# Longformer attention with a StarReLU feed-forward on one core: bias pieces in plain rows, and three transfers and turns moved

## The chip, the core and the metric

One Trainium2 chip, one of its cores. The metric is the device time of the program in microseconds, as the median of the runs; a profiled execution of the same program has its own time, which stands below beside its span.

## What is computed

For 8 batch elements of 8 heads, 576 positions and 64 columns, attention is taken within a window of 32 positions on either side and with 8 global positions; its output, with the heads side by side, is the input of a feed-forward of 512 to 2048 to 512 columns with the activation s * relu(h)^2 + b.

```python
scores = scale * np.matmul(q, k.transpose(0, 1, 3, 2))
mask = np.abs(pos[:, None] - pos[None, :]) <= window
mask = mask | is_global[:, None] | is_global[None, :]
...
attn = np.exp(scores)
attn = attn / (np.sum(attn, axis=-1, keepdims=True) + 1e-09)
x = np.matmul(attn, v)
...
h = x @ w_in
r = np.maximum(h, 0.0)
g = s * (r * r) + b
out = g @ w_out
```

The constant b reaches the output as b times the column sums of w_out. The kernel forms these sums by itself, and this is the "bias" of the title.

## The kernel before, in words

**Tiles and stages.** Two heads make a pair; there are 32 pairs, counted from 0, four to a batch element. Keys lie in 5 tiles of 120 rows plus the 8 global ones; each pair has two score steps (`qk(p, 0)` and `qk(p, 1)`, L652) whose products go through an exponential on ACT (L659) and a mask product on DVE (L660), and the products with V (`pvq`, L676) follow a step later. The feed-forward runs beside it on the same PE: `moe_quanta` is a generator whose steps (L771 into the hidden layer, L812 out of it) are put between the attention's steps by `run_pair`, eight steps to a pair. The work is bf16 with sums in f32.

**What sets the order.** All engines are in a manual schedule: each engine runs its instructions in the order in which the program writes them. Tables of (pair, step) say at which step a transfer or a copy is written. From pair 8 on PE's score work for pair p and the first half for pair p+1 stand together in `visit(p)`, which from pair 12 on is at step 3 of the pair.

**Q and K on their way.** For pairs 1 to 8 POOL loads K and Q with a cast (`load_kq`, L209) into a ring of five slots, and PE turns them (`trans`, L601). From pair 9 on SP loads K (`load_nat`, L236), ACT rounds it to bf16 (L247) and SP issues a DMA transposition (`turn_k`, L307) at step 5 of pair j-3; DVE then copies the global keys into it (`put_kq`, L566). From pair 18 on Q goes the same way (`load_q`, L264; `turn_q`, L312). All of these stand in SP's one queue in program order. At step 0 of pair 14 SP has the loads for pair 19, at step 4 those for pair 20, at step 5 the transposition of K of pair 17. A tile of K or Q rows has 64 f32 per row, so 256 bytes in one run. V of pairs 16 and later is loaded by POOL with a cast (L236, `vring`), its global rows by L555.

**The bias.** `w_out` is 4 MB in f32. `wpiece(j)` (L1146) has POOL load 512 KB, 128 partitions with a row of 1024 f32, into buffer `wst[j % 2]`; pieces 2 to 7 add themselves to what lies there (`accum_op`). Two pieces each are written at step 6 of pairs 11, 12, 14 and 15. `wadd` (L1152) then has DVE add the four halves in three additions in pair 17, and `bias` (L1158) multiplies the result with ones in pair 18.

**The other places.** `scatter(0, 1)` copies the global rows' results into place, eight small copies on POOL (L748); `load_kq(6)` is written behind it. `turned(trans_b, 5)` writes the turns of Q of pair 5 on PE and keeps their copy (L631) for later; it stands behind both score steps of pair 4. `gather(1)` (L405) fetches the global rows of K and Q of the second batch elements, two indirect transfers, and `load_kq(8)` stands behind it.

Of the kernel before, what the change touches and what calls it, by code (L numbers as in the profile page):

```python
# [9 lines left out]
FP32 = mybir.dt.float32  # L10
BF16 = mybir.dt.bfloat16
AF = mybir.ActivationFunctionType
OP = mybir.AluOpType
# [3 lines left out]
P = 128  # L17
# [3 lines left out]
DM, DF = 512, 2048  # L21
# [33 lines left out]
VGLOBAL = {  # L55
    8: (8, 3), 9: (8, 4), 10: (8, 7), 11: (9, 6), 12: (10, 6), 13: (11, 7), 14: (12, 7), 15: (13, 7),
}
KT0 = 16
NX = 3
N6 = NCH * KC // NJ  # L60
# [33 lines left out]
def kernel(  # L94
# [12 lines left out]
    nc = tc.nc  # L107
# [13 lines left out]
    stage = ctx.enter_context(tc.tile_pool(name="stage", bufs=1))  # L121
# [76 lines left out]
    wsum = wpool.tile([P, DM], FP32)  # L198
# [4 lines left out]
    w_in2 = moe_w_in.rearrange("(g p h) f -> p g h f", g=2, h=2)  # L203
    w_out2 = moe_w_out.rearrange("(a p t) n -> p a (t n)", p=P, t=2)

    def load_kq(p):
        bi, hp = divmod(p, 4)
        for t in "kq":
            nc.gpsimd.dma_start(  # L209
                out=six[t][:NP6, p % NR].rearrange("p h j d -> p h (j d)"),  # L210
                in_=src[t][bi, 2 * hp : 2 * hp + 2].rearrange("h (p j) d -> p h (j d)", j=NJ),
            )
# [186 lines left out]
    def gather(bb, ts="kq"):  # L399

        if bb not in gfs:
            gfs[bb] = globp.tile([P, 3, D], FP32, tag="gf", name="gf")
        for t in ts:
            i = "kqv".index(t)
            nc.gpsimd.indirect_dma_start(  # L405
                out=gfs[bb][:, i], out_offset=None,
                in_=src[t].rearrange("b h s d -> (b h s) d"),
                in_offset=IndirectOffsetOnAxis(ap=grow[bb][:], axis=0),
            )
# [97 lines left out]
    def flush():  # L507
        ops, later[:] = list(later), []
        for f in ops:
            f()  # L510
# [60 lines left out]
    both = [None]  # L571

    def trans(t, p):
        if p == 4:
            if t == "k":
                both[0] = ps_s.tile([P, 2, DM], FP32, tag="s", name="pst")
            ps = both[0][:, "kq".index(t)].bitcast(BF16)[:, 0:LQ]
        elif p < 5 or (t == "k" and p > 5):
            ps = bank("pst").bitcast(BF16)[:, 0:LQ]
        elif t == "k":  # L580
            ps = rings[-1].tile([P, DM], FP32, tag="moe", name="pst")[:].bitcast(BF16)[:, 0:LQ]
        else:
            both[0] = ps_s.tile([P, 2, DM], FP32, tag="s", name="pst")
            ps = both[0][:, 0].bitcast(BF16)[:, 0:LQ]
        if p >= NSIXQ:
            for c in range(NCH):
                nc.tensor.transpose(
                    ps[:, P * c : P * c + KC], qnat(p)[0:KC, P * c : P * c + P],
                    ident[0:KC, 0:KC],
                )  # L590
            return ps
        for j in range(NJ):
            n = N6 if j == NJ - 1 else NP6
            if t == "q" and p >= NSIX:
                nc.tensor.transpose(
                    ps[:, NP6 * j : NP6 * j + n],
                    qrow(p)[:n, j].rearrange("p h d -> p (h d)"), ident[:n, :n],
                )
                continue
            for hh in range(2):  # L600
                nc.tensor.transpose(  # L601
                    ps[D * hh : D * hh + D, NP6 * j : NP6 * j + n],
                    six[t][:n, p % NR, hh, j], ident[:n, :n],
                )
        return ps
# [138 lines left out]
    def scatter(bi, g=None):  # L744

        h = slice(0, 4) if g is None else slice(2 * g, 2 * g + 2)
        for i in range(NG):
            nc.gpsimd.tensor_copy(  # L748
                out=xt[:, h, S * (bi % NX) : S * (bi % NX) + S][:, :, ds(greg_p[i], 1)],
                in_=xgs[bi][:, h, i : i + 1],  # L750
            )
# [225 lines left out]
    def turned(f, p):  # L977
        ops = []
        f(p, ops)
        return ops[0]  # L980
# [113 lines left out]
    flush()  # L1094
    q_out()
    k_out()
    scatter(0, 1)
    load_kq(6)
    load_w_in(1, (1,))
    load_kq(7)  # L1100
    load_w_out(0)
# [15 lines left out]
    qk(4, 0)  # L1117
    lead()
    flush()
    steps0[0]()  # L1120
    qk(4, 1)
    flush()
# [3 lines left out]
    load_v(nc.sync, 7)  # L1126
    load_nat(nc.sync, "k", 9)
    load_q(9)
    q_out = turned(trans_b, 5)
    steps0[1]()  # L1130
    g_out = later.pop()
    q_out()
# [2 lines left out]
    flush()  # L1135
    cast_v(A, 4)
    gvall = const.tile([NG, (B - 2) * H * D], BF16)
    gather(1)
    load_kq(8)
    load_w_out(3)  # L1140
    quanta[0] = 31

    wst = [stage.tile([P, 2, DM], FP32, name=f"wst{i}", tag=f"wst{i}") for i in range(2)]

    def wpiece(j):
        nc.gpsimd.dma_start(  # L1146
            out=wst[j % 2][:].rearrange("p t n -> p (t n)"), in_=w_out2[:, j],
            **({"accum_op": OP.add} if j > 1 else {}),
        )

    def wadd(i):
        nc.vector.tensor_add(  # L1152
            out=wsum[:], in0=wsum[:] if i else wst[0][:, 0], in1=wst[(i + 1) // 2][:, (i + 1) % 2]
        )

    def bias():
        ps = bank("psb")
# [8 lines left out]
    for p in range(4, NPAIR):  # L1166
# [3 lines left out]
        def at(s, f, *a, ex=ex):  # L1170
            ex.setdefault(s, []).append(lambda: f(*a))
# [71 lines left out]
            at(4, steps[1])  # L1243
        elif p % 8 == 5 and 8 < p < NPAIR - 3:
            at(1, steps[1])
        if p in (11, 12, 14, 15):
            for j in range(2):
                at(6, wpiece, 2 * (11, 12, 14, 15).index(p) + j)
        if p == 17:
            for j in range(3):  # L1250
                at(2 * j + 2, wadd, j)
        if p == 18:
            at(2, bias)
        if p > 18 and hp in (0, 3) and held_rows:
# [46 lines left out]
```

## Time and profile before

| | |
|---|---|
| median of 3 runs | 343.88 us (342.3 to 344.29) |
| the profiled execution's own time | 343.63 us |
| its span, first to last instruction | 341.6 us |
| busy: PE, DVE, ACT, POOL | 322.5 (94%), 200.8 (59%), 199.7 (58%), 119.2 (35%) us |
| mean granted clock of PE | 0.98 |
| DMA | 125609 packets, 49.54 MB; 114072 of them under 512 B |

The page's times are microseconds from the first instruction. An engine's busy share is a mean over stages with different limits. A wait is time in which an engine stood idle, with what ended it. The queue q1 holds what SP issues, q0 what POOL issues; both use the same 16 DMA engines. A share of 16 engines can exceed 100%, since the time of every packet is counted from its start to its end.

### The profile page before, as it was taken

How to read it: one execution, taken by the hardware profiler on the slowest of the kernel's cores; microseconds unless marked ns; L12 is line 12 of the kernel's file. 1: busy time of each engine (PE TensorE's matmuls, PEld its weight loads, DVE VectorE, ACT ScalarE, POOL GpSimd, SP SyncE). 2: the span in 40 equal slices, each digit the busy share in tenths (PEclk: the TensorE clock that was granted, in tenths of full speed). 3: DMA queues.
4: the chain of work that ended last, by engine and by line, in shares of the span. 5: the costliest groups of instructions: out<-in, count | busy, mean ns of one | idle time of the engine just before them, and what ended most of it. 6: DMA issues, size and time to landing. Idle time of an engine off the chain costs nothing.

```text
span 341.6 us, 8778 instructions
## 1 busy us (share of the span) xinstructions
PE 322.5 (94%) x3403; PEld 169.5 (50%) x3403; DVE 200.8 (59%) x526; ACT 199.7 (58%) x335; POOL 119.2 (35%) x228
## 2 busy tenths in 40 slices
PE   7998999999999991699999999999999999999996
PEld 5754444444545450357744444444467544444444
DVE  6876686767786760347765676567656534423422
ACT  4777776578947871527865886588358505503600
POOL 7287624424235340080447605840670030000000
PEclk9999999999999997599999999999999999999999
DMA  8999999999999999899979999992950011011002
GB/s 145 195 179 219 203 208 216 191 205 167 251 196 178 111 195 181 147 173 162 165 154 249 189 179 187 238 166 53 203 114 2 2 68 57 0 61 63 0 34 92
DMA packets 125609, 49.54 MB, mean 145 GB/s; under 512 B 114072, under 2 KB 119640, under 8 KB 125560
## 3 DMA queue, kind: packets, MB, share of 16 engines
q1 hardware_dynamic: 94030, 27.49, 46.7%
q0 software_dynamic: 31184, 21.07, 37.3%
q8 instruction: 27, 0.44, 0.5%
q10 hardware_dynamic: 354, 0.43, 0.4%
q14 instruction: 14, 0.11, 0.1%
HBM read 42.28 MB, written 9.44 MB: 151 GB/s over the span
## 4 chain that ended last, share of the span: by engine, by line
PE 77%; DMA 9%; SPq 6%; POOL 3%; DVE 2%; issue 2%; ACT 1%; POOLq 0%; ACTq 0%
PE pso L812 35%; PE psh L771 31%; PE po L676 6%; DMA natq<-in_q_dram 4%; DMA sixk<-in_k_dram 3%; SPq L264 3%; SPq L236 2%; PE pss L652 2%; PE psw L652 1%; DMA natv<-in_v_dram 1%; PE pst L601 1%; DMA kt<-natb 1%; POOL xt L748 1%; DVE xt L723 1%; POOL gf L405 1%
## 5 line engine op out<-in xcount | busy, mean ns | idle before, releaser
L812 PE MATMUL pso<-wout_t,g 128*128 128x512 bf16 (+1 forms) x592 | 131.7, 378 | 0.0
L771 PE MATMUL psh<-xt,win 128*128 128x512 bf16 (+2 forms) x704 | 131.1, 341 | 0.3 <-DMA win<-in_moe_w_in_dram 0.3
L794 ACT ACTIVATE r<-psh 128x512 bf16<-128x512 f32 x144 | 85.7, 599 | 58.5 <-PE psh L771 53.2
L771 PEld LDWEIGHTS <-win 128*128 128x128 bf16 x704 | 63.2, 98 | 57.2 <-issue 0.6
L812 PEld LDWEIGHTS <-g 128*128 128x128 bf16 x592 | 56.5, 98 | 64.8 <-issue 3.0
L797 DVE TENSOR_TENSOR g<-r 128x512 bf16<-128x512 bf16 x144 | 61.0, 429 | 37.7 <-ACT r L794 35.3
L660 DVE TENSOR_TENSOR em<-em,mask 128x904 bf16<-128x904 bf16 x64 | 39.2, 616 | 35.1 <-ACT em L659 32.8
L659 ACT ACTIVATE em<-pss 128x840 bf16<-128x840 f32 (+1 forms) x38 | 33.5, 882 | 37.9 <-PE pss L652 37.6
L236 POOL DMA_DIRECT2D vring<-in_v_dram x33 | 30.6, 967 | 13.6 <-PE psh L771 8.7
L834 DVE SCALAR_TENSOR_TENSOR osb<-pso,sb,bias_row 128x512 f32<-128x512 f32 (+1 forms) x25 | 18.2, 728 | 28.7 <-PE pso L812 28.4
L723 DVE TENSOR_TENSOR xt<-po,rep 128x480 bf16<-128x480 f32 (+2 forms) x60 | 24.5, 450 | 3.8 <-ACT rep L733 3.8
L748 POOL COPY xt<-xg 128x4 bf16 (+1 forms) x72 | 16.4, 228 | 28.2 <-DVE xt L723 24.3
L652 PEld LDWEIGHTS <-kt 64*128 64x128 bf16 x384 | 12.1, 99 | 26.5 <-issue 12.3
L659 ACT ACTIVATE em<-psw 128x904 bf16<-128x904 f32 x23 | 21.2, 923 | 3.2 <-PE psw L652 3.2
L838 POOL DMA_DIRECT2D out_dram<-osb x16 | 9.1, 569 | 30.8 <-DVE osb L834 25.4
L676 PE MATMUL po<-em,vring 128*32 128x160 bf16 (+3 forms) x840 | 18.8, 224 | 0.7 <-issue 0.5
L322 POOL CAST vring<-natv 128x640 bf16<-128x640 f32 x10 | 8.0, 797 | 32.6 <-DMA natv<-in_v_dram 31.9
L247 ACT CAST natb<-natk 128x640 bf16<-128x640 f32 x22 | 15.9, 722 | 5.3 <-DMA natk<-in_k_dram 3.4
L652 PE MATMUL psw<-qt,kt 64*128 64x160 bf16 (+1 forms) x138 | 8.5, 230 | 10.1 <-DVE kt L566 10.0
L730 ACT ACTIVATE ln<-po 128x324 f32<-128x324 f32 (+1 forms) x30 | 12.9, 429 | 5.4 <-PE po L676 5.4
L652 PE MATMUL pss<-qt,kt 64*128 64x192 bf16 (+4 forms) x228 | 14.6, 240 | 1.5 <-ACT em L659 0.5
L676 PEld LDWEIGHTS <-vring 128*32 128x32 bf16 x896 | 14.6, 101 | 1.4 <-issue 1.3
(127 smaller groups left out, 253.5 us busy)
## 6 DMA issues: line engine op xcount, KB each, us to landing
natk<-in_k_dram SPq DMA_DIRECT2D x45, 150.0 KB
natv<-in_v_dram SPq DMA_DIRECT2D x28, 150.0 KB
natq<-in_q_dram SPq DMA_DIRECT2D x55, 75.0 KB
wst<-in_moe_w_out_dram POOLq DMA_DIRECT2D x8, 512.0 KB, 6.0
out_dram<-osb POOLq DMA_DIRECT2D x16, 256.0 KB, 4.1
natq<-in_q_dram SPq DMA_DIRECT2D x9, 288.0 KB
vring<-in_v_dram POOLq DMA_DIRECT2D x31, 75.0 KB, 5.3
out_dram<-osbh POOLq DMA_DIRECT2D x9, 256.0 KB
```

The lines of the kernel that those rows point to most:

```text
L236: eng.dma_start(out=dst[r : r + rows, n, c : c + nch, hh], in_=bass.AP(tensor=src[t].tensor, offset=o + c * KC * D, ap=[[D, rows], [KC * D ...
L652: nc.tensor.matmul(ps[:, hh, at : at + hi - lo], ktile[p][r, P * c : P * c + P], qbufs[p % 3][r, lo:hi], start=at == 0, stop=at + hi - lo ...
L659: nc.scalar.activation(em[:], ps[:, :, 0:n], AF.Exp, scale=SCALE)
L660: later.append(lambda: nc.vector.tensor_mul(em[:], em[:], masks[g]))
L676: nc.tensor.matmul(po[DH * j : DH * j + DH, a : a + n], view(vring[:, p % NVR, c, hh, part - 1 :], [2, DH]) if part else onesb[:], emt[(p, ...
L723: nc.vector.tensor_tensor(out=view(xt[:, 2 * g, x0 + t0 :], [NXT, 2], [w, runs], [1, w]), in0=view(po[:, STEP[blk] + col :], [STEP[blk], 2 ...
L748: nc.gpsimd.tensor_copy(out=xt[:, h, S * (bi % NX) : S * (bi % NX) + S][:, :, ds(greg_p[i], 1)], in_=xgs[bi][:, h, i : i + 1],)
L771: nc.tensor.matmul(psh[:, d0 : d0 + n], win_t[f // 8][:, a, 2 * P * (f % 8 // 2) :][:, 0 : 2 * P] .rearrange("p (x t) -> p t x", t=2)[:, f ...
L794: nc.scalar.activation(r[:], psh, AF.Relu)
L797: later.append(lambda g=g, r=r: nc.vector.tensor_mul(g[:], r[:], r[:]))
L812: nc.tensor.matmul(pso[:, 0:nn], gl[f][:, u * P : u * P + P], wout_t[:, f, n0 : n0 + nn], start=(f == 0), stop=(f == 15),)
L834: nc.vector.scalar_tensor_tensor(out=osb[:, 0:nn], in0=pso[:, 0:nn], scalar=s_bc, in1=bias_row[:, n0 : n0 + nn], op0=OP.mult, op1=OP.add,)
```

## The change

The eight pieces of 512 KB become sixteen of 256 KB, 128 partitions with a row of 512 f32, four to a set, in four buffers, and none adds itself to anything. A table `WPIECES` says at which (pair, step) a set is issued, and at which steps its four additions stand on DVE; there are fifteen additions, all into `wsum`. The first set is issued at step 1 of pair 11 and added in pair 12, the second at step 5 of pair 12 and added in pair 14, the third at step 4 of pair 14 and added in pair 15 and at step 0 of pair 16, the fourth at step 0 of pair 16 and added in pair 17. Besides, POOL's load of K of pair 6 stands ahead of `scatter(0, 1)`, that of Q behind it; the turns of Q of pair 5 stand between the two score steps of pair 4 and go into another PSUM tile; and `load_kq(8)` stands ahead of `gather(1)`.

```diff
--- before.py
+++ after.py
@@ -55,6 +55,12 @@
 VGLOBAL = {
     8: (8, 3), 9: (8, 4), 10: (8, 7), 11: (9, 6), 12: (10, 6), 13: (11, 7), 14: (12, 7), 15: (13, 7),
 }
+WPIECES = [
+    ((11, 1), ((12, 0), (12, 1), (12, 2), (12, 4))),
+    ((12, 5), ((14, 0), (14, 1), (14, 2), (14, 4))),
+    ((14, 4), ((15, 5), (15, 6), (15, 7), (16, 0))),
+    ((16, 0), ((17, 1), (17, 2), (17, 4), (17, 5))),
+]
 KT0 = 16
 NX = 3
 N6 = NCH * KC // NJ
@@ -203,9 +209,9 @@
     w_in2 = moe_w_in.rearrange("(g p h) f -> p g h f", g=2, h=2)
     w_out2 = moe_w_out.rearrange("(a p t) n -> p a (t n)", p=P, t=2)
 
-    def load_kq(p):
+    def load_kq(p, which="kq"):
         bi, hp = divmod(p, 4)
-        for t in "kq":
+        for t in which:
             nc.gpsimd.dma_start(
                 out=six[t][:NP6, p % NR].rearrange("p h j d -> p h (j d)"),
                 in_=src[t][bi, 2 * hp : 2 * hp + 2].rearrange("h (p j) d -> p h (j d)", j=NJ),
@@ -580,7 +586,11 @@
         elif t == "k":
             ps = rings[-1].tile([P, DM], FP32, tag="moe", name="pst")[:].bitcast(BF16)[:, 0:LQ]
         else:
-            both[0] = ps_s.tile([P, 2, DM], FP32, tag="s", name="pst")
+            if p == 5:
+                both[0] = ps_o.tile([P, 2 * DM], FP32, tag="o", name="pst")
+                both[0] = both[0][:].rearrange("p (h x) -> p h x", h=2)
+            else:
+                both[0] = ps_s.tile([P, 2, DM], FP32, tag="s", name="pst")
             ps = both[0][:, 0].bitcast(BF16)[:, 0:LQ]
         if p >= NSIXQ:
             for c in range(NCH):
@@ -1094,8 +1104,9 @@
     flush()
     q_out()
     k_out()
+    load_kq(6, "k")
     scatter(0, 1)
-    load_kq(6)
+    load_kq(6, "q")
     load_w_in(1, (1,))
     load_kq(7)
     load_w_out(0)
@@ -1117,6 +1128,7 @@
     qk(4, 0)
     lead()
     flush()
+    q_out = turned(trans_b, 5)
     steps0[0]()
     qk(4, 1)
     flush()
@@ -1126,7 +1138,6 @@
     load_v(nc.sync, 7)
     load_nat(nc.sync, "k", 9)
     load_q(9)
-    q_out = turned(trans_b, 5)
     steps0[1]()
     g_out = later.pop()
     q_out()
@@ -1135,23 +1146,22 @@
     flush()
     cast_v(A, 4)
     gvall = const.tile([NG, (B - 2) * H * D], BF16)
+    load_kq(8)
     gather(1)
-    load_kq(8)
     load_w_out(3)
     quanta[0] = 31
 
-    wst = [stage.tile([P, 2, DM], FP32, name=f"wst{i}", tag=f"wst{i}") for i in range(2)]
-
-    def wpiece(j):
-        nc.gpsimd.dma_start(
-            out=wst[j % 2][:].rearrange("p t n -> p (t n)"), in_=w_out2[:, j],
-            **({"accum_op": OP.add} if j > 1 else {}),
-        )
-
-    def wadd(i):
-        nc.vector.tensor_add(
-            out=wsum[:], in0=wsum[:] if i else wst[0][:, 0], in1=wst[(i + 1) // 2][:, (i + 1) % 2]
-        )
+    wst = [stage.tile([P, DM], FP32, name=f"wst{i}", tag=f"wst{i}") for i in range(4)]
+
+    def wpieces(j):
+        for i in range(4):
+            nc.gpsimd.dma_start(out=wst[i][:], in_=w_out2[:, 2 * j + i // 2, DM * (i % 2) :][:, 0:DM])
+
+    def wadd(j, i):
+        if j + i == 0:
+            return
+        a, b = (wsum, wst[i]) if j or i > 1 else wst[0:2]
+        nc.vector.tensor_add(out=wsum[:], in0=a[:], in1=b[:])
 
     def bias():
         ps = bank("psb")
@@ -1243,12 +1253,12 @@
             at(4, steps[1])
         elif p % 8 == 5 and 8 < p < NPAIR - 3:
             at(1, steps[1])
-        if p in (11, 12, 14, 15):
-            for j in range(2):
-                at(6, wpiece, 2 * (11, 12, 14, 15).index(p) + j)
-        if p == 17:
-            for j in range(3):
-                at(2 * j + 2, wadd, j)
+        for j, (x, adds) in enumerate(WPIECES):
+            for i, y in enumerate(adds):
+                if y[0] == p:
+                    at(y[1], wadd, j, i)
+            if x[0] == p:
+                at(x[1], wpieces, j)
         if p == 18:
             at(2, bias)
         if p > 18 and hp in (0, 3) and held_rows:
```

POOL's order from the scatter of the third batch element (pairs 12 to 16) on, before: `wst` are the bias pieces, `vring<-in_v_dram` V of pairs 16, 17 and 18, `vring<-gvall` their global rows.

```order
L1146 DMA wst_1041<-in_moe_w_out_dram 128x1024
L1146 DMA wst_1042<-in_moe_w_out_dram 128x1024
L236 DMA vring<-in_v_dram 120x5x64 x2
L1146 DMA wst_1041<-in_moe_w_out_dram 128x1024
L1146 DMA wst_1042<-in_moe_w_out_dram 128x1024
L555 DMA vring<-gvall 8x5x128
L236 DMA vring<-in_v_dram 120x5x64 x2
L1146 DMA wst_1041<-in_moe_w_out_dram 128x1024
L1146 DMA wst_1042<-in_moe_w_out_dram 128x1024
```

And now:

```order
L242 DMA vring<-in_v_dram 120x5x64 x2
L1158 DMA wst_1041<-in_moe_w_out_dram 128x512
L1158 DMA wst_1042<-in_moe_w_out_dram 128x512
L1158 DMA wst_1043<-in_moe_w_out_dram 128x512
L1158 DMA wst_1044<-in_moe_w_out_dram 128x512
L561 DMA vring<-gvall 8x5x128
L242 DMA vring<-in_v_dram 120x5x64 x2
L561 DMA vring<-gvall 8x5x128
L1158 DMA wst_1041<-in_moe_w_out_dram 128x512
L1158 DMA wst_1042<-in_moe_w_out_dram 128x512
L1158 DMA wst_1043<-in_moe_w_out_dram 128x512
L1158 DMA wst_1044<-in_moe_w_out_dram 128x512
```

The two pieces that stood between the scatter and V of pair 16 are now four ahead of the scatter; the third set stands where the second pair of pieces stood; the fourth stands behind the global rows that it stood ahead of.

DVE's order in pair 14, before: `qt` and `kt` are the copies for the visit of the same pair, `g` the squares of the feed-forward, `em` the mask products.

```order
L566 COPY qt_117<-gqt_121 128x5x8
L797 TENSOR_TENSOR g_2490<-r 128x512
L797 TENSOR_TENSOR g_2514<-r 128x512
L566 COPY kt<-gkt 128x5x8
L797 TENSOR_TENSOR g_2526<-r 128x512
L797 TENSOR_TENSOR g_2535<-r 128x512
L660 TENSOR_TENSOR em_2543<-em_2543,mask_449 128x840
L660 TENSOR_TENSOR em_2556<-em_2556,mask_441 128x904
```

And now:

```order
L572 COPY qt_117<-gqt_121 128x5x8
L807 TENSOR_TENSOR g_2499<-r 128x512
L1164 TENSOR_TENSOR wsum<-wsum,wst_1041 128x512
L807 TENSOR_TENSOR g_2524<-r 128x512
L572 COPY kt<-gkt 128x5x8
L1164 TENSOR_TENSOR wsum<-wsum,wst_1042 128x512
L807 TENSOR_TENSOR g_2537<-r 128x512
L1164 TENSOR_TENSOR wsum<-wsum,wst_1043 128x512
L807 TENSOR_TENSOR g_2547<-r 128x512
L670 TENSOR_TENSOR em_2555<-em_2555,mask_449 128x840
L670 TENSOR_TENSOR em_2568<-em_2568,mask_441 128x904
```

One addition stands ahead of the copy of K, three ahead of the mask products.

## Rows read from the trace of the kernel before

**Rows 1.** PE's waits: engine, line and tile, what ended the wait: total, times, longest.
```profile
PE psw L652 <- DVE kt L566: 10.0, 1, 10.0
...
PE pst L601 <- DMA sixk<-in_k_dram: 0.4, 1, 0.4
```
**Rows 2.** The chain that ended last: start, us, engine, tile, line, count.
```profile
96.17 0.20 PE psw L652 x6
96.37 0.67 PE po L676 x36
...
136.14 3.04 DMA kt<-natb
...
139.44 0.56 PE psw L652 x5
139.99 1.17 PE po L676 x38
141.16 9.11 PE pso L812 x32
...
242.88 7.01 PE pso L812 x32
```
**Rows 3.** Timeline of SP's queue, 72 to 142: start, us, line, transfer, count.
```profile
110.85 2.69 SPq L236 DMA_DIRECT2D natk<-in_k_dram  x2
113.58 11.30 SPq L264 DMA_DIRECT2D natq<-in_q_dram  x4
124.93 5.84 SPq L236 DMA_DIRECT2D natk<-in_k_dram  x2
130.88 5.09 SPq L264 DMA_DIRECT2D natq<-in_q_dram  x4
...
138.63 1.92 SPq L264 DMA_DIRECT2D natq<-in_q_dram  x4
```
**Rows 4.** Timeline of POOL, 100 to 142; in brackets idle time before, and what ended it.
```profile
99.73 0.72 POOL L322 CAST vring<-natv 128x640 bf16<-128x640 f32 x1 [5.32 <-DMA natv<-in_v_dram]
...
113.41 0.85 POOL L1146 DMA_DIRECT2D wst<-in_moe_w_out_dram  x1 [3.45 <-DMA wst<-in_moe_w_out_dram]
...
125.54 0.85 POOL L1146 DMA_DIRECT2D wst<-in_moe_w_out_dram  x1 [3.08 <-DMA natq<-in_q_dram]
```
**Rows 5.** Slices of 1 us: length, PE busy, granted clock, DMA share, GB/s.
```profile
131.00:132.00 1.00, 0.00 (x0) 0.86 1.17 196
...
145.00:146.00 1.00, 1.00 (x5) 0.82 0.93 211
```
**Rows 6.** DMA queues in 106 to 109: packets, MB, share of 16 engines.
```profile
q0 software_dynamic: 139, 0.50, 86.9%
```
**Rows 7.** DMA queues in 88 to 89.
```profile
q0 software_dynamic: 62, 0.25, 86.2%
```
**Rows 8.** DMA queues in 310 to 330.
```profile
q1 hardware_dynamic: 235, 0.45, 5.9%
```
**Rows 9.** DMA queues in 138 to 144.
```profile
q1 hardware_dynamic: 3679, 0.90, 89.8%
```
**Rows 10.** All DMA packets in 123 to 126.
```profile
DMA packets 2171, 0.51 MB, mean 168 GB/s; under 512 B 2137, under 2 KB 2145, under 8 KB 2171
```
**Rows 11.** All DMA packets in 117 to 119.
```profile
DMA packets 39, 0.10 MB, mean 51 GB/s; under 512 B 15, under 2 KB 15, under 8 KB 39
```
**Rows 12.** Timeline of DVE, 106 to 128.
```profile
120.52 0.18 DVE L566 COPY kt<-gkt 128x40 bf16<-128x40 bf16 x1 [0.50 <-DMA kt<-natb]
```
**Rows 13.** Instructions that touch `wst`: duration in ns, smallest, median, largest.
```profile
L1152 DVE TENSOR_TENSOR wsum<-wsum,wst x2: 681/684/686, 153.5 to 155.7; 128x512 f32<-128x512 f32 x2
```
**Rows 14.** Slice of 4 us: length, busy PE, PEld, DVE, ACT, POOL, clock, DMA share, GB/s.
```profile
116.00:120.00 4.00, 4.00 (x25) 1.93 (x24) 3.48 (x10) 2.67 (x6) 0.73 (x1) 1.00 0.57 81
```
**Rows 15.** DMA issues of the page: count, KB each, median us to landing.
```profile
wst<-in_moe_w_out_dram POOLq DMA_DIRECT2D x8, 512.0 KB, 6.0
```
**Rows 16.** DMA issues in 114 to 120.
```profile
vring<-in_v_dram POOLq DMA_DIRECT2D x2, 75.0 KB, 12.5
```

## The prediction

> Pairs are counted from 0 here, as in the code: the title's 6th pair is pair 5. Each four of the sixteen pieces are called a set.
>
> **What bounds the kernel now.** The page first: PE is busy for 94% of the span, so only what stops PE, or slows it, costs time. The second view is PE's list of waits [rows 1]: one wait of 10.0 us is nearly all that there is to take, and the next that bears on the change is 0.4 us. The third is the chain of waits followed back from that stop [rows 2]: `psw` at 139.44 waits for K of pair 17. SP issued its DMA transposition at 136.14, the data took 3.04 us, DVE's small copy about 0.2 us. PE had nothing to do from about 129.46 (139.44 less 9.98), so an issue by 126.2, 9.9 us earlier, would have cost nothing.
>
> Why was SP so late? Its own timeline [rows 3] shows what stands ahead of that issue: the K and Q loads of pairs 19 and 20. Four Q issues take 1.92 us where nothing disturbs them (the row at 138.63); here they took 11.30 and 5.09 us, and two K issues 2.69 and 5.84 us. An issue that takes so long, with no other engine named as the one waited for, goes into a queue that does not drain. POOL's timeline [rows 4] shows what shares the 16 DMA engines with it: accumulating 512 KB pieces of `moe_w_out`, three of the six between 113 and 126 (the first and the last stand in the rows), the first of them held up until an earlier piece of its buffer had landed.
>
> The clock comes last [rows 5]: it falls from 1.00 to 0.50 of full speed (2.4 to 1.2 GHz) inside the slice 131 to 132, when PE had stood still since 129.46, and is back inside 145 to 146, with PE at work since 139.44. So nearly 6 us of work after the stop run at half clock.
>
> **The change, part by part.**
>
> *Accumulation removed, pieces halved.* In 106 to 109 the software queue moved 139 packets, all but a few of 4 KB, at 86.9% of 16 engines [rows 6]: 0.869 x 16 x 3 us / 139 = 300 ns each, accumulating. In 88 to 89 4 KB without accumulation took 0.862 x 16 x 1 us / 62 = 222 ns [rows 7]. The new pieces are 2 KB rows without accumulation, and no row has such a load. Bounds: 80 ns, a packet of an output store with rows of 2 KB (0.059 x 16 x 20 us / 235, [rows 8]), and 222 ns, if half the bytes were no cheaper. I take 111 ns, half of the 4 KB row, which is the nearest: same tensor, same direction, same queue. 1 MB then costs all engines 256 x 300 / 16 = 4.8 us before and 512 x 111 / 16 = 3.6 us now (2.6 to 7.1).
>
> *What that does to SP's queue.* From 110.85 to 136.14, 25.3 us, SP pushes four times 300 KB, 4,800 packets of 256 B. The hardware queue alone moves 3,679 packets in 6 us, 613 in one [rows 9]; beside a V load with its 128 B packets the two queues move 2,171 in 3 us, 724 in one [rows 10]. Before: four accumulating pieces (512 packets of 300 ns over 16 engines), 9.6 us; the V load's 1,200 packets beside as many of SP's, 2,400 / 724 = 3.3 us; the other 3,600 alone, 5.9 us; together 18.8 us. Some 6.5 us are left over, and part of them is a stretch in which hardly anything moves, 39 packets in 117 to 119 [rows 11]. After: only the third set lies there, 3.6 us, since the fourth is released by additions that stand from step 5 of pair 15 on, from about 123. With 3.3 and 5.9 us that is 12.8 us: the turn of K is issued at 123.6, 2.6 us before it is needed. With the dear packet (222 ns) it is issued at 127.1, 0.9 us late; if the thin stretch returns with 4 us, at 127.6, 1.4 us late; with both, 5 us late. I take no stop, **-9.98 us**, because the nearest row for the packet leaves a margin, and keep the 5 us for the range.
>
> *The sets' places.* The second set now falls near 97 instead of 103, into a stretch that the queues already fill. Most exposed is the K copy of pair 16 at 120.52, which waited 0.50 us for its transposition [rows 12]; what lay ahead of that was the old second megabyte and the first accumulations of the third. Both now come earlier or cost less, so I cost the move at nothing; without that cover this copy is late first, a visit of PE before the old stop.
>
> *Clock.* Without the stop nothing lets it fall. At half clock `psw`, `po` and 32 `pso` took 0.56 + 1.17 + 9.11 us, the same blocks at full clock 0.20 + 0.67 + 7.01 [rows 2]: **-2.96 us**, and nothing of it if 5 us of stop stay.
>
> *Fifteen additions instead of three.* Twelve more at 0.68 us [rows 13] are 8.2 us of DVE, in pairs 12 and 14 to 17; DVE has 3.48 of 4 us filled in the fullest stretch there [rows 14]. PE feels it only where a copy that it waits for stands behind an addition; one addition stands ahead of the K copy in pair 14. I take **+0.3 us**, half of one addition, between 0 and 2.5 us (one set's four with no gap for them). On POOL, eight more issues of at most 0.85 us; behind the second set's four, which wait for DVE, stand the cast of V and a scatter, and POOL stood idle for 5.32 us before that cast [rows 4]. That idle time hides them: 0.
>
> *K of pair 6 ahead of the scatter.* PE waited 0.4 us for it [rows 1]; POOL now issues it before eight column copies. **-0.4 us**, between 0 (the weights issued ahead of it in the same queue land first) and 0.8 us (as much again behind it). *Q of pair 5 turned between the score steps of pair 4; K and Q of pair 8 ahead of the gather.* The transposition fills a hole of PE, but DVE copies its result in the same place, behind the second mask product, so PE meets the next wait: 0, between -0.4 and +0.4 us. The gather moves behind two loads of 144 KB and is rounded much later.
>
> **Sum.** 341.6 - 9.98 - 2.96 - 0.4 + 0.3 = 328.6 us of span. The profiled execution took 343.63 us, 2.03 us over its span, which makes **330.6 us**. It lay 0.25 us under the median of the runs shown, 343.88.
>
> The trace has 6.0 us from issue to landing of a plain 512 KB piece [rows 15]. A rule of the Trainium skill speaks against cutting it in two: "DMA: Bandwidth & Descriptors", sections "Anatomy of one DMA — SWDGE (gpsimd) path" and "Rules for kernel authors", asks for transfers of 1 MiB and more and counts about 2.0 us fixed plus the bytes at 436 GB/s for each. As an estimate from that page, four pieces of 256 KB one after another take 10.4 us where two of 512 KB take 6.4 us, and the sum would grow by what DVE waits for them, as in the third rival.
>
> **The rivals.**
> 1. *The stop shrinks but stays.* Nothing in the trace names the cause of the thin stretch [rows 11]; if the V load makes it, and not the accumulation, it returns. With the dear packet as well: 5 us of stop and the clock's 3 us: 330.6 + 8 = **338.6 us**, or anything from 333.5 to 341.
> 2. *The change does not do what it says*: SP is late by its own small packets, and the new pieces hold the engines as long as the old. That is so from 150 ns for half the bytes if the thin stretch stays in full. For it: 4,800 packets are there as before. Against it: 111 ns as half of the plain row. Only the 0.4 us and the additions are left: **343.5 us**.
> 3. *Slower: DVE becomes the wait.* DVE works in order, and a set's additions stand ahead of mask products and K copies. The third set's last piece is issued near 114 and its first addition stands near 123: from about 9 us to landing on, DVE stops, and ACT and PE behind it. For it: a 75 KB software load took 12.5 us in this stretch [rows 16]. Against it: 6.0 us for 512 KB [rows 15]. At 12.5 us it is 3.5 us for each of the last two sets, with the old stop only moved: 343.5 + 7 = **350 us**.
>
> By the page's 10.4 us the third rival would be just past its point.
>
> **How the numbers follow.** Forecast (328.5 to 333.5): 0.66, as the margin of 2.6 us hangs on one price taken between bounds. The first rival 0.16, the second 0.10, the third 0.08. A measurement of this kernel tells some 0.5%, 1.7 us, from no change. Faster by more: forecast and first rival, 0.82; the same: the second, 0.10; slower: the third, 0.08. The range takes in the forecast and the first rival and leaves out the other two: 328.5 to 341.
>
> **What would show it.** Right: PE's list without the 10.0 us; four Q issues of SP near 2 us in 113 to 131; the turn of K issued near 124; the clock at 1.00 from 30 to the end; PE's 0.4 us for K gone. Wrong: a `psw` that still waits for a K copy, at this pair or a neighbour; DVE rows that wait for `wst`; a PE wait for a copy that an addition held up.

## The result, and the profile after

Over four runs the change took 334.37 us in the median (331.49 to 339.33) beside 344.0 us of the kernel before: a ratio of 0.9702, 95% interval 0.9613 to 0.9791. It is faster, as forecast; the time forecast was 330.6 us, the range 328.5 to 341. The profiled execution took 331.49 us, with a span of 329.9. A second series gave 334.24 us (six runs, 330.99 to 339.78), ratio 0.9685 [0.9628, 0.9742]. Two single times near 339.5 us are left out of these ratios, and no profile shows one of them.

First PE's list of waits in the change, of the same columns as [rows 1]:

```profile
PE psw L662 <- DVE kt L572: 1.6, 2, 1.4
...
PE pss L662 <- DVE g L807: 0.8, 1, 0.8
PE psw L662 <- DVE gqt L539: 0.6, 1, 0.6
```

The 10.0 us of [rows 1] are gone, and so are the 0.4 us of `pst`. The three lines shown are new, all short. The first is two waits, for K of pair 9 near 67 and for K of pair 10 near 75; the 0.8 us stand at 34.05, where PE is no later than before (34.03); the 0.6 us stand near 105 and are taken up in run 7. SP's timeline shows why the long one went; it answers to [rows 3]:

```profile
112.99 1.00 SPq L242 DMA_DIRECT2D natk<-in_k_dram  x2
114.04 1.97 SPq L270 DMA_DIRECT2D natq<-in_q_dram  x4
116.05 1.04 SPq L242 DMA_DIRECT2D natk<-in_k_dram  x2
117.21 3.99 SPq L270 DMA_DIRECT2D natq<-in_q_dram  x4
121.36 1.92 SPq L313 DMA_TRANSPOSE kt<-natb  x1
```

The same four issues that took 2.69, 11.30, 5.84 and 5.09 us now take 1.00, 1.97, 1.04 and 3.99. The transposition of K of pair 17 is issued at 121.36 instead of 136.14. POOL's timeline, beside [rows 4], shows when the third and the fourth set are issued:

```profile
113.19 0.58 POOL L1158 DMA_DIRECT2D wst<-in_moe_w_out_dram  x1 [6.58 <-DVE wsum L1164]
...
117.58 0.54 POOL L1158 DMA_DIRECT2D wst<-in_moe_w_out_dram  x1 [1.90 <-DVE wsum L1164]
...
126.06 0.58 POOL L1158 DMA_DIRECT2D wst<-in_moe_w_out_dram  x1 [4.87 <-DVE wsum L1164]
```

Between 118 and 126 no piece is issued: the fourth set's buffers come free only with the third set's additions. The stretch 117 to 119, in which 39 packets moved before [rows 11], now moves 667:

```profile
DMA packets 667, 0.51 MB, mean 253 GB/s; under 512 B 577, under 2 KB 577, under 8 KB 667
```

The clock, in the windows that answer to [rows 5] (length, busy PE, PEld, DVE, ACT and POOL, clock, DMA share, GB/s), stays at 1.00:

```profile
130.00:132.00 2.00, 1.84 (x56) 1.20 (x56) 0.73 (x3) 1.29 (x2) 1.43 (x2) 1.00 1.14 253
132.00:146.00 14.00, 13.84 (x135) 8.67 (x135) 10.74 (x27) 8.92 (x17) 8.60 (x17) 1.00 1.44 204
```

Where the 11.7 us of span came from is read off PE's timeline, by the starts of the score blocks. The rows of the change, with idle time before them in brackets:

```profile
65.15 0.36 PE L662 MATMUL pss<-qt,kt 64*128 64x92 bf16 x6
66.92 0.37 PE L662 MATMUL psw<-qt,kt 64*128 64x160 bf16 x6 [1.42 <-DVE kt L572]
...
104.14 0.36 PE L662 MATMUL pss<-qt,kt 64*128 64x92 bf16 x6
105.10 0.37 PE L662 MATMUL psw<-qt,kt 64*128 64x160 bf16 x6 [0.60 <-DVE gqt L539]
...
130.31 0.36 PE L662 MATMUL pss<-qt,kt 64*128 64x92 bf16 x6
130.50 0.36 PE L662 MATMUL psw<-qt,kt 64*128 64x160 bf16 x6
```

Before, these six stood at 66.22, 66.69, 103.67, 103.86, 129.10 and 139.44, the last two being the stop:

```profile
129.10 0.36 PE L652 MATMUL pss<-qt,kt 64*128 64x92 bf16 x6
139.44 0.56 PE L652 MATMUL psw<-qt,kt 64*128 64x160 bf16 x6 [9.98 <-DVE kt L566]
```

So PE is 1.07 us ahead at 65.15 and gives that back at once (+0.23 at 66.92), is 0.47 us behind at 104.14, 1.24 us behind after the wait at 105.10, 1.21 us behind at 130.31. From there to the next block it needs 0.19 us where it needed 10.34: 10.15 us gained. After that block it gains 2.76 more (8.94 ahead, 11.7 at the end). All of that is there by the next block (138.48 instead of 150.20), the stretch that ran at half clock before, so it is the clock. Sum: 1.21 - 10.15 - 2.76 = -11.7 us.

### The profile page after: what moved, and what is told of

Its sections match the earlier page's. It is cut to its first block, busy times and chain, and to the rows that moved or that the text cites. A ratio compares the mean times of both kernels' runs of the same rounds, so it can differ in the third digit from the quotient of the medians.

```text
span 329.9 us, 8781 instructions
## 1 busy us (share of the span) xinstructions
PE 315.7 (96%) x3366; PEld 168.4 (51%) x3403; DVE 208.1 (63%) x538; ACT 199.6 (61%) x335; POOL 121.6 (37%) x236
## 4 chain that ended last, share of the span: by engine, by line
PE 80%; DMA 9%; ACT 4%; DVE 3%; issue 2%; SPq 1%; ACTq 0%; DVEq 0%
PE psh L781 34%; PE pso L822 32%; PE po L686 6%; DMA natk<-in_k_dram 5%; DMA kt<-natb 4%; PE pss L662 3%; ACT em L669 2%; PE pst L611 1%; PE psw L662 1%; PE psf L985 1%; SPq L242 1%; ACT r L804 1%; DVE xt L733 1%; PE psf L964 1%; PE pst L605 0%
## 5 line engine op out<-in xcount | busy, mean ns | idle before, releaser
L781 PE MATMUL psh<-xt,win 128*128 128x512 bf16 (+4 forms) x688 | 129.7, 340 | 1.1 <-issue 0.3
L822 PE MATMUL pso<-wout_t,g 128*128 128x512 bf16 (+1 forms) x573 | 126.4, 373 | 2.4 <-issue 2.1
L242 POOL DMA_DIRECT2D vring<-in_v_dram x33 | 29.4, 895 | 12.6 <-PE psh L781 7.2
L758 POOL COPY xt<-xg 128x4 bf16 (+1 forms) x72 | 17.2, 238 | 12.7 <-DVE xt L733 8.7
L1158 POOL DMA_DIRECT2D wst<-in_moe_w_out_dram x16 | 8.9, 573 | 19.6 <-DVE wsum L1164 16.5
```

The costliest lines, as they stand in the source:

```text
L242: eng.dma_start(out=dst[r : r + rows, n, c : c + nch, hh], in_=bass.AP(tensor=src[t].tensor, offset=o + c * KC * D, ap=[[D, rows], [KC * D ...
L758: nc.gpsimd.tensor_copy(out=xt[:, h, S * (bi % NX) : S * (bi % NX) + S][:, :, ds(greg_p[i], 1)], in_=xgs[bi][:, h, i : i + 1],)
L781: nc.tensor.matmul(psh[:, d0 : d0 + n], win_t[f // 8][:, a, 2 * P * (f % 8 // 2) :][:, 0 : 2 * P] .rearrange("p (x t) -> p t x", t=2)[:, f ...
L822: nc.tensor.matmul(pso[:, 0:nn], gl[f][:, u * P : u * P + P], wout_t[:, f, n0 : n0 + nn], start=(f == 0), stop=(f == 15),)
```

## The experiments

Eleven runs followed: 1 to 4 on one chip, 5, 6, 7 and 10 on a second, 8, 9 and 11 on a third, each group beside the kernel before.

**1. The accumulation alone, at the old places** (the kernel before with one line out; a later piece of a buffer then overwrites the earlier one):

```diff
-            **({"accum_op": OP.add} if j > 1 else {}),
```

> The kernel before with the accumulation alone taken away: the same eight pieces of 512 KB, at the same steps, with the same waits for the earlier piece of the buffer, each overwriting what lay there (so the bias is that of the last pieces alone). My theory, that the accumulating packets hold the DMA engines and SP's queue behind them: PE's 10.0 us wait for K of pair 17 and the half clock are gone, span 328 to 332 us, time 330 to 334 us, a 4 KB packet of these pieces near 220 ns instead of 300. Rival, that the smaller pieces or the new steps did it: the wait stays at 8 us or more, time 341 to 345 us.

Measured: 337.54 us (336.96 to 338.11), ratio 0.9803 [0.9736, 0.987]. The stop is still there, shorter, and the transposition is issued at 124.20:

```profile
PE psw L652 <- DVE kt L566: 4.7, 2, 4.4
```
```profile
118.62 5.41 SPq L264 DMA_DIRECT2D natq<-in_q_dram  x4
124.20 2.57 SPq L307 DMA_TRANSPOSE kt<-natb  x1
```

The chain of this profile gives the transposition's time from issue to landing, 8.77 us where it was 3.04 before [rows 2]:

```profile
124.20 8.77 DMA kt<-natb
```

Plain pieces bring 6 us of the gain, not all of it: between the two expectations. The turn is issued 2 us before the 126.2 that the prediction asks for, and PE still stops for 4.43 us.

**2. The three other moves alone** (the change with the old bias load, whose core is):

```diff
-            nc.gpsimd.dma_start(out=wst[i][:], in_=w_out2[:, 2 * j + i // 2, DM * (i % 2) :][:, 0:DM])
+            out=wst[j % 2][:].rearrange("p t n -> p (t n)"), in_=w_out2[:, j],
+            **({"accum_op": OP.add} if j > 1 else {}),
```

> The kernel before with the three moves (K of pair 6 ahead of the scatter, Q of pair 5 between the score steps of pair 4, K and Q of pair 8 ahead of the gather) and the old bias. My theory: the moves are worth next to nothing: the first wait for K of pair 6 (0.4 us) goes, PE is up to 0.9 us ahead near 44 us and 0.3 to 0.5 us behind the kernel before from about 75 us on, where a copy of K of pair 9 is late; the 10 us wait stays; time 342.5 to 345 us. Rival, that the moves carry a share of the gain: 340 us or less.

Measured: 344.14 us (342.6 to 344.88), ratio 0.9982 [0.9947, 1.0018]: no difference. The new wait at 67 is there as in the change, so it belongs to the moves. It is for K of pair 9, the first that SP turns (the expectation has that wait near 75):

```profile
67.02 0.37 PE L662 MATMUL psw<-qt,kt 64*128 64x160 bf16 x6 [1.56 <-DVE kt L572]
```

**3. The bias pieces alone** (the change with those three moves undone):

```diff
...
-    load_kq(6, "k")
     scatter(0, 1)
-    load_kq(6, "q")
+    load_kq(6)
...
-    q_out = turned(trans_b, 5)
     steps0[0]()
...
+    q_out = turned(trans_b, 5)
     steps0[1]()
...
-    load_kq(8)
     gather(1)
+    load_kq(8)
```

> The changed kernel with its three moves undone. My theory: the bias pieces carry the whole gain: no wait of 10 us, clock 1.0, span 328.5 to 330.5 us, time within 1.5 us of the changed kernel and rather below it, since the 1.4 us wait near 75 us goes with the moves. Rival, that the moves were needed: 334 us or more in its best run.

Measured: 335.95 us (332.89 to 337.61), ratio 0.9745 [0.9655, 0.9836]: the whole gain, within the intervals. Its profiled span of 334.0 us is not the 328.5 to 330.5 expected. PE waits there 2.3 us for the first weights (`win`, at 28.36), with the clock at 0.50 at 31, and so begins the score block at 31.06 that the change begins at 29.34. It has no wait near 67, but at the place of the 0.60 us a longer one:

```profile
107.52 0.37 PE L658 MATMUL psw<-qt,kt 64*128 64x160 bf16 x6 [2.50 <-DVE gqt L539]
```

**4. The new steps with accumulation** (the change's pieces, steps and buffers; sets two to four accumulate, three additions on DVE):

```diff
+                **({"accum_op": OP.add} if j else {}),
...
-        if j + i == 0:
+        if j < 3 or i == 0:
             return
-        a, b = (wsum, wst[i]) if j or i > 1 else wst[0:2]
+        a, b = (wsum, wst[i]) if i > 1 else wst[0:2]
```

> The changed kernel with the sets 2 to 4 adding themselves to their buffers in the DMA and three additions on DVE at the end: the same sixteen pieces, buffers and steps of the change, waits for the landed piece instead of for DVE. My theory: accumulation costs about a third to a half more per packet, and the wait of PE for a K copy in pairs 14 to 17 is back with 4 to 10 us, the clock falls again, time 337 to 345 us. Rival, that the steps and the four buffers made the gain: no wait over 2 us, time 330 to 335 us.

Measured: 339.7 us (339.44 to 341.15), ratio 0.9878 [0.9809, 0.9948], inside the theory's 337 to 345. The stop at the old block is back, with its clock (the block takes 0.56 us again):

```profile
137.11 0.56 PE L662 MATMUL psw<-qt,kt 64*128 64x160 bf16 x6 [4.75 <-DVE kt L572]
```

The pieces did not go out at the change's times, though. An accumulating set waits for no addition on DVE, so the third and the fourth are issued 6 and 7 us earlier than in the change (113.19 and 126.06), and both lie ahead of the turn of K:

```profile
107.11 3.60 POOL L1158 DMA_DIRECT2D wst<-in_moe_w_out_dram  x4
118.84 3.63 POOL L1158 DMA_DIRECT2D wst<-in_moe_w_out_dram  x4
```

Their packets are dear as well. In 114 to 116 the software queue moved 188 packets and 0.35 MB, about 2 KB each, at 94.6% of 16 engines: 0.946 x 16 x 2 us / 188 = 161 ns, so 512 x 161 / 16 = 5.2 us for a megabyte.

Runs 1 and 4 with the two kernels make a table of medians in us (not all of one series, so good to about 1 us):

| | accumulating | plain |
|---|---|---|
| old steps | 344.0 | 337.5 |
| new steps | 339.7 | 334.4 |

The upper row differs by one line of code: plainness is worth 6.5 us there. The right column differs in the steps, in the wait for DVE, in the size of a piece and in the moves, together 3.1 us; for the last two, runs 2, 3 and 5 show nothing clear of noise. The lower row is not plainness alone, since its sets are issued at different times.

**5. Eight pieces of 512 KB at the new places** (plain, the same steps and fifteen additions):

```diff
...
-        for i in range(4):
-            nc.gpsimd.dma_start(out=wst[i][:], in_=w_out2[:, 2 * j + i // 2, DM * (i % 2) :][:, 0:DM])
+        for i in range(2):
+            nc.gpsimd.dma_start(out=wst2[i][:].rearrange("p t n -> p (t n)"), in_=w_out2[:, 2 * j + i])
```

> The change with eight plain pieces of 512 KB (rows of 4 KB) in place of sixteen of 256 KB (rows of 2 KB), at the same steps, with the same fifteen additions. Theory (what counts is that nothing accumulates and that each megabyte comes when the queue has room; the packets that carry the small pieces are of 4 KB as well, about 170 ns each near 102): the waits for K stay under 2.5 us and the time is 331 to 338 us, that of the change. Rival (the small pieces carry the gain that a plain load of the old pieces did not give): the stop at K of pair 16 or 17 comes back with 2 to 5 us and the time is 336 to 341 us.

Measured: 335.65 us (333.53 to 337.41), ratio 0.9774 [0.9714, 0.9834], which overlaps the change's in the same series. The waits for K stay under 2 us, as the theory has it, and no stop at K of pair 16 or 17 comes back: small pieces aren't what took it away. Its profile waits 1.49 us for Q of pair 18. The ratios leave room for some 3 us against the larger pieces.

**6. The change once more**, not edited.

> The change once more, for the spread of its times beside the other runs of this call. Theory (a wait near 105 that is of another length in each execution, with a fall of the clock when it is long): median 331 to 336 us, single times up to 339, and a wait for K of pair 14 of between 0 and 3 us in the profile. Rival (the spread is of the chip and not of this wait): the wait is 0.6 us again, whatever the time.

Measured: 334.24 us, as told above; this profiled execution took 335.76 us with a span of 334.1, 4.2 us longer than the first. PE's rows show where:

```profile
104.69 0.36 PE L662 MATMUL pss<-qt,kt 64*128 64x92 bf16 x6
107.59 0.37 PE L662 MATMUL psw<-qt,kt 64*128 64x160 bf16 x6 [2.55 <-DVE gqt L539]
117.58 0.36 PE L662 MATMUL pss<-qt,kt 64*128 64x92 bf16 x6
```

At 107.59 it is 2.5 us behind the first execution, at 117.58 4.2 us: the clock fell behind the stop (length, busy PE, clock, DMA share, GB/s):

```profile
109.00:112.00 3.00, 3.00 (x8) 0.50 1.40 141
```

Of the 4.2 us, 0.55 were lost before the block (104.69 for 104.14), 1.95 are the longer wait (2.55 us for 0.60) and 1.70 the clock behind it. So this one wait makes most of the difference between the two.

**7. The second set later**, behind POOL's cast and copies:

```diff
-    ((12, 5), ((14, 0), (14, 1), (14, 2), (14, 4))),
+    ((13, 0), ((14, 0), (14, 1), (14, 2), (14, 4))),
```

> The change with one row of its table altered: the second set is issued at the start of pair 13 instead of in step 5 of pair 12, so that POOL issues it behind a cast and eight column copies, near 105 instead of 97. Theory (what is left of the change's waits near 105 comes from the second set: its four pieces run ahead of the tail of the transposition of K of pair 14): PE's wait of 0.6 us, and of 2.5 us in the run with the bias alone changed, is gone; the span is 0.5 to 1.5 us under the change's 329.9, the time 330 to 333 us, and the runs lie closer together than 331 to 339. Rival A (the wait is due to SP's own K and V loads ahead of that transposition): the wait stays at 0.5 to 2.5 us and the times are those of the change, 331 to 339. Rival B (the new place only hands the harm on): the transposition of K of pair 15 or 16 lands late, PE waits for it 1 to 4 us at 112 or 121, time 334 to 340 us.

Measured: 332.97 us (331.81 to 337.01), ratio 0.9695 [0.9649, 0.9741]. The wait near 105 is gone (`psw` at 104.59). It was a wait for K of pair 14, whose copy waited for its transposition in the change; the profile names `gqt`, a copy that DVE makes just behind it. The copy stood at 104.67 there, at 107.17 in run 6, and stands at 103.21 here with no wait. First the change, then this run:

```profile
104.67 0.18 DVE L572 COPY kt<-gkt 128x40 bf16<-128x40 bf16 x1 [1.44 <-DMA kt<-natb]
```
```profile
103.21 0.16 DVE L572 COPY kt<-gkt 128x40 bf16<-128x40 bf16 x1
```

The span is 331.0 us, not the 0.5 to 1.5 us below 329.9 that the theory has. A wait for Q of pair 18 is there that the change's two profiles don't have:

```profile
139.79 0.37 PE L662 MATMUL psw<-qt,kt 64*128 64x160 bf16 x6 [1.20 <-DVE qt L572]
```

Run 5, whose second set was not moved, has one of 1.49 us, so this run doesn't show that its move made it. The cause of the wait near 105 is shown by all profiles together: it stands where the second set is issued near 97 (0.60 and 2.55 us, 2.50 in run 3, 0.78 in run 4), is 0.16 us with the set at 98.61 (run 5), and is not there with the set at 103 or later (runs 7 to 10) or without it (run 11). The 1.3 us gained in the median lie inside the intervals. Windows of the change's DMA queues show what moves meanwhile. The transposition is issued at 96.62 and lands 8.04 us later. In 100.5 to 101.3 hardly anything moves, the second set's pieces, issued from 96.98 on, included; then they fill the engines (first 100.5 to 101.3, then 101.4 to 103):

```profile
DMA packets 60, 0.02 MB, mean 19 GB/s; under 512 B 60, under 2 KB 60, under 8 KB 60
...
DMA packets 296, 0.62 MB, mean 388 GB/s; under 512 B 152, under 2 KB 152, under 8 KB 296
...
q0 software_dynamic: 176, 0.59, 97.5%
```

**8. The fourth set written four steps later as well**, beside the edit of run 7:

```diff
-    ((16, 0), ((17, 1), (17, 2), (17, 4), (17, 5))),
+    ((16, 4), ((17, 4), (17, 5), (17, 6), (17, 7))),
```

> The change with two rows of its table altered: the second set issued at the start of pair 13 (as in the run before), and the fourth set issued in step 4 of pair 16 instead of step 0, its additions in steps 4 to 7 of pair 17. Theory (in the run with the second set late the only wait left was 1.2 us for Q of pair 18, whose transposition was issued at 131.64, took 7.75 us and lay among the fourth set's packets): that wait goes, no wait for K of pair 14 comes back, span 329 to 330.5 us, median 330.5 to 332.5 us. Rival (the transposition is held by SP's own loads of pair 21): the 1.2 us stay and the median is that of the run before, 333 us. Second rival: the fourth set now holds the transpositions of pair 19, a wait of 1 to 3 us near 147, median 334 to 336 us.

Measured: 333.46 us (332.69 to 336.03), ratio 0.9708 [0.9671, 0.9745]. Q of pair 18 is in time, but the profile stops for K of pair 17 again, whose transposition was issued at 125.64:

```profile
132.74 0.37 PE L662 MATMUL psw<-qt,kt 64*128 64x160 bf16 x6 [2.07 <-DVE kt L572]
```

The edit did not move the set: its pieces wait for the third set's additions on DVE and go out from 126.07 on, as in the change (126.06). What it moved is POOL's load of V of pair 18, which now stands ahead of them, at 121.17 instead of 131.11, and the additions of the set:

```profile
121.17 1.81 POOL L242 DMA_DIRECT2D vring<-in_v_dram  x2
126.07 0.58 POOL L1158 DMA_DIRECT2D wst<-in_moe_w_out_dram  x1 [3.09 <-DVE wsum L1164]
```

The transposition of K of pair 17 landed 6.85 us after its issue. So the run tests none of its expectations; what a later fourth set would do stays open.

**9. The second set later, the three moves undone**: the edits of runs 3 and 7 together.

> The change's bias pieces with the second set at the start of pair 13, and the three other moves (Q of pair 5, K of pair 6, the gather) undone. Theory (those moves are worth nothing, since what PE gains by 44 us it waits for K of pair 8 near 67): no wait near 105, median 331.5 to 334 us, within 0.5% of the run with the second set late alone. Rival (the moves are worth their 0.4 to 0.9 us once the later stop is gone): median 0.5 to 1.5 us above that run, 333.5 to 334.5 us.

Measured: 332.53 us (331.1 to 334.55), ratio 0.9668 [0.9634, 0.9703], the lowest of all that compute the same; it beats the kernel before, but is not told apart from the change. No worth of the moves shows here either. Its profile, of the slowest of its six runs, waits 2.94 us for Q of pair 18, so that one is of varying length too (1.20 us in run 7).

**10. Every addition twice** (the second into a tile that nothing reads):

```diff
...
+        nc.vector.tensor_add(out=wscr[:], in0=wst[0][:], in1=b[:])
```

> The change with each of the fifteen additions followed by a second one of the same size into a tile that nothing reads: 15 x 0.68 = 10.3 us more of DVE. Theory (DVE has room in these pairs, and PE feels an addition only where a copy for PE stands behind it): 0.3 to 2.5 us more than the change, 332 to 337 us. Rival (the additions are on the path): most of the 10.3 us appear, 340 to 345 us.

Measured: 336.4 us (335.92 to 337.12), ratio 0.9787 [0.9739, 0.9836]: 2.2 us above the change's median in the same series, inside the theory's 0.3 to 2.5; the two intervals just meet. It is not the price of the additions alone, since the doubled ones release the second set later too, at 103.52, and the wait near 105 is gone. Beside run 7, whose second set is as late, it is 3.4 us. The waits at K of pairs 15 to 17 (0.22, 0.39 and 1.67 us) are for short copies; the longest is held up behind additions:

```profile
PE psw L662 <- DVE kt L572: 4.3, 5, 1.7
```
```profile
134.27 0.68 DVE L1166 TENSOR_TENSOR wsum<-wsum,wst 128x512 f32<-128x512 f32 x1
134.87 0.68 DVE L1167 TENSOR_TENSOR wscr<-wst,wst 128x512 f32<-128x512 f32 x1
135.47 0.17 DVE L572 COPY kt<-gkt 128x40 bf16<-128x40 bf16 x1
```

**11. Only the first set loaded:**

```diff
-            if x[0] == p:
+            if x[0] == p and j == 0:
                 at(x[1], wpieces, j)
```

> The change with the first of the four sets alone loaded (the bias row then sums wrong pieces; the fifteen additions are all made): what the other three megabytes still cost. Theory (what is left of their cost is the wait near 105 and the fall of the clock behind it, in some executions): no wait for K of pair 14, SP's K of pair 17 turned by 119, single times all within 330 to 333 us. Rival (the spread does not come from these loads): times spread over 331 to 339 us as before.

Measured: 331.28 us (329.45 to 331.44), ratio 0.9626 [0.958, 0.9672]. The times lie closely together, one of them just below the 330 to 333 of the theory, and K of pair 17 is turned at 117.42. The bias is wrong here, as in run 1, since pieces are missing. So the other three megabytes cost the change some 3 us in the median (334.24 less 331.28; 2 us by the ratios, whose intervals overlap). Four times within 2 us, where the change's six spread over 9, point to them as the cause of its spread.

## Why the prediction was right, point by point

**The bound and its cause: right.** PE's long wait was SP's late issue, and that was a queue that did not drain beside POOL's pieces: the turn of K is issued at 136.14 before, at 124.20 without accumulation (run 1), at 117.42 with the first set alone (run 11). Of the stop 10.15 us went (term: 9.98), of the clock 2.76 (term: 2.96).

**The margin: two errors that cancelled, which was luck.** The turn was forecast at 123.6 and said to be needed by 126.2. That deadline took the landing from the one row of 3.04 us. Beside more traffic it took longer: issued at 124.20 it landed 8.77 us later and PE stopped for 4.43 us (run 1), issued at 125.64 it took 6.85 us and PE waited 2.07 (run 8). With run 1's landing, 123.6 would have been 2 to 3 us late. On the other side SP's queue drained faster than in the sum: from the first of its four issues to the turn it took 8.37 us (112.99 to 121.36) and not 12.8. A megabyte priced too dear (3.6 us for 2.8, below) is 0.8 of these 4.4 us; what the rest is stays open.

**The price of a piece: inside its bounds, wrong in its working.** I halved the 4 KB packet to get 111 ns for rows of 2 KB. In 101.4 to 103 the software queue moved 176 packets; the 144 of 2 KB and more carry nearly all of 0.59 MB, so 4 KB each: two rows went in one packet. 0.975 x 16 x 1.6 us / 144 is 173 ns at most for 4 KB, where accumulating took 300 [rows 6]. One megabyte is 256 x 173 / 16 = 2.8 us, not the 3.6 of the term. The Trainium skill, "DMA: Bandwidth & Descriptors", section "SWDGE vs HWDGE vs iDMA", says of a packet that it is preferably at most 4096 B and may hold several descriptors; the trace agrees with 4 KB here, while run 4's accumulating pieces of the same rows went as 2 KB.

**Which half does what: the working told it, and the two halves were not priced apart.** The 12.8 us after consisted of cheaper pieces and of fewer of them in the stretch ("only the third set lies there"). Run 1 has plain pieces with two megabytes between 110 and 125 and still stops for 4.43 us: cheap pieces alone do not do it. Run 4 has two megabytes there too, dear ones, and stops for 4.75. No run accumulates at the times of the change, so that the places alone would not do it is argued and not shown.

**The step that failed: the sets' places, costed at nothing.** I looked at the old second megabyte's cover and named the K copy of pair 16 as late first. It was the copy of pair 14: the transposition that the second set now runs into, at 96.62, was not looked at for its own landing, only the stretch as "already full". It costs 0.60 us in one profile, and in the other 1.95 us more and 1.70 us of the clock's fall behind it. The profiled span is 1.3 us above the sum: PE is 1.21 us behind at 130.31, where the sum has moves and additions at -0.1, and 0.77 of that appear at the block near 105. The wait is most of what separates the profiled 331.49 us, the fastest of its four runs and 0.9 above the forecast of 330.6, from the 335.76 of run 6. The median of 334.4 lies between, just above the forecast's own 328.5 to 333.5; that the profiled one came so near 330.6 is luck of the execution. What each execution without a profile waited isn't known, but without the second and later sets (run 11) no single time is above 331.44. The first rival's range (333.5 to 341) holds the median, but its mechanism, a remnant of the old stop from a dear packet, did not occur in either profile of the change. The second rival's condition (150 ns and the thin stretch in full) gives by the prediction's own sum a turn at 131.4, 5 us late as in the first rival, and not the whole stop that its 343.5 us count.

**The moved loads: the wait went, the gain didn't stay.** K of pair 6 was to give 0.4 us. With the moves PE reaches the block at 65.15 us 1.07 us early and waits 1.42 us there for K of pair 9; without them (run 9) it reaches it at 66.11 and waits for nothing. The term did not ask what is late next. (The expectation of run 9 calls that wait K of pair 8; its copy waits for a DMA transposition, which K has from pair 9 on.)

**The additions: perhaps low.** I took 0.3 us of 0 to 2.5 for twelve. Fifteen more on top cost 2.2 us beside the change and 3.4 beside run 7, 0.15 to 0.23 us for each 0.68 us; at that price twelve would be 1.8 to 2.7 us, which is an upper estimate, since DVE has less room in run 10. In the change's own profile no wait of PE for a K copy is due to an addition: the copies of pairs 9, 10 and 14 waited for their transpositions. The third rival fell: no row of DVE waits for `wst`.

**The rule on large transfers.** The Trainium skill's counsel of 1 MiB and more ("DMA: Bandwidth & Descriptors", "Rules for kernel authors") would have spoken for run 5. There a piece of 512 KB lands in 6.6 us in the median, one of 256 KB in 5.3 in the change, DVE waits for a piece in neither, and the times are not told apart: no gain of the larger piece is shown here.

## What to carry to other kernels

Price a background load not by its bytes but by the transfers that it runs into: list every transposition and load whose consumer stands within a few us of its landing, and ask of each new place which of them it now crosses. When a load is moved clear of one deadline, read the next ones on the same queues: here waits for K of pair 14 and for Q of pair 18 stood behind the one that went. Take the landing of a transfer that the margin hangs on from more than one row: 3.04 us here was 8.77 in run 1. And read in the trace when a moved transfer goes out before you say what the run shows: in runs 4 and 8 other waits set the time, not the step. Where one execution beats its own median by 3 us, take a second profile before accounting for the gain.

## What was not expected of the hardware

- Accumulating 4 KB took 300 ns of an engine [rows 6], plain 222 [rows 7] or 173 ns at most. The stretch of 39 packets in 2 us [rows 11] did not come back there without accumulation, but that is not shown to be its cause: run 4 accumulates and has none in 110 to 125, and run 9 has plain pieces and 40 packets, 0.04 MB, in 133 to 135. Why so little moved is not settled.
- In 100.5 to 101.3 of the change, and of run 7, 60 and 33 packets moved although a transposition had been issued some 4 us before and, in the change, the second set's first pieces as well; no run isolates the cause.
- A transposition of K took from 3.04 us (before, K of pair 17) to 10.07 us (run 6, K of pair 14) from issue to landing.
- Stops of PE of 0.60, 1.20 and 1.76 us (the last in run 5) left the clock at 1.00. Those of 2.07, 2.50, 2.55 and 2.94 us had it at 0.50 in some of the slices behind them, and a wait of 2.55 us so cost 3.6 us more than one of 0.60.
